# Output blocks of the third batch moved around the last attention, with another PE order

## The chip, the cores and the metric

The kernel runs on one core of one Trainium2 chip. The metric is the device time of one execution in microseconds. A core has TensorE (PE, with its weight loads as PEld), VectorE (DVE), ScalarE (ACT), GpSimd (POOL) and SyncE (SP), which issues the DMAs.

## What is computed

Inputs are q, k and v of 4 batches, 12 heads, 448 positions and 64 columns, in float32. Three stages follow one another in each batch:

```python
# 1: attention, causal, 12 heads -> x (448 x 768)
scores = q @ k.T / sqrt(64); scores[above the diagonal] = -1e9
x = softmax(scores) @ v
# 2: mixing of tokens and channels
theta = x @ w_theta
y = w_tok_r @ (x * cos(theta)) + w_tok_i @ (x * sin(theta))
u = x + y
x = u + relu(u @ w_ch)
# 3: four experts, each a causal attention; two per token count, by the gate
logits = x @ w_gate; w = softmax over the two largest of 4
out = sum over e of w[e] * (softmax(x wq[e] (x wk[e]).T / 8) @ (x wv[e])) @ wo[e]
```

## The kernel before, in words

Data lie transposed: 768 channels are six tiles of 128 partitions, 448 positions are the columns. Float32 products that have to be exact are made of a high and a low part in a rounded format, with three matmuls (high x high, high x low, low x high). Four kinds of work are recorded per batch b: `attn1` (a0 to a3: six pairs of heads, in three groups of two), `mixing` (m), `project` (p: the channel product, the queries and keys of the experts, the values and the gate) and `attn2` (c: two pairs of experts, then six output blocks).

Nothing is issued while it is recorded. `Plan` (line 187 on) keeps each operation as a step with what it reads and writes. PE's steps fall into 268 numbered places (`plan.next()`), and the list `RUNS` (line 568) says in which order PE takes them: (11,16) is the next 16 steps of place 11. `rank` derives a due time for every other step from PE's line, and `issue` runs a list schedule with these due times, in which it also chooses the engine of a step that has a choice (`copy` and `scale`, lines 302 to 316) and the buffer of each tile. The numbers in `K` (line 566) are margins of that schedule. Each engine then runs its instructions in the order so found.

Places that the text speaks of: 29 and 31 are mixing blocks of batch 0. 55 is the scores of the last 64 queries of the third group of `attn1(1)`, 57 the transposes of P of its last pair, 106 the first score place of `attn1(2)`. 171 is a mixing block of batch 2, 195 and 199 channel blocks behind it; 238 is the mixing block of batch 3's fifth tile and 241 a channel block. 214 and 215 are P times V of the third batch's `attn2`, 216 to 221 its output blocks. 251 to 254 are the values and the gate of batch 3, 255 to 257 the scores of the last `attn2`, 258 and 259 its transposes, 260 and 261 P times V, 262 to 267 its output blocks.

An output block (`attn2`, line 1064) is six matmuls with the attention output's high and low parts (`hl`), one eviction to SBUF (`ob`) by ScalarE or VectorE, and one store. Its weights are loaded into one of 4 buffers `c1` (for the last batch, of 6 buffers `unit`). In `two` (line 813) the gate enters through `norm` (line 762): the reciprocal of each row's sum is multiplied by the gate, and each tile of P is scaled by it before it is transposed by PE and copied from PSUM to SBUF. In `attn2` that scaling can run on GpSimd or ScalarE:

```python
    def scale(self, out, p, by, engines="gs"):
...
                plan.scale(p, p, rec[:, col:col + 1])
...
            hl = [sbt([S], F32R, "hc") for _ in range(2)] if x.dest is None else []
...
            ob = sbt([S], F32, "xt" if b == B - 1 else "cmb")
```

Pools have fixed numbers of buffers: hc 4, cmb 2, zt 10 (the pool of z), xt 12 (the pool of x). Two pairs of an `attn2` take all four of hc.

Of the kernel before, what the change touches and what calls it, by code (L numbers as in the profile page):

```python
# [12 lines left out]
F32 = mybir.dt.float32  # L13
F32R = mybir.dt.float32r
# [6 lines left out]
B, H, S, D = 4, 12, 448, 64  # L21
# [108 lines left out]
class Plan:  # L130
# [206 lines left out]
    def rank(self, last):  # L337
# [22 lines left out]
        for s in reversed(self.steps):  # L360
            if s.engine != "tensor":
# [3 lines left out]
                if s.engine == "sync":  # L365
                    s.after = max(0.0, s.due - K["ahold"])
        for group in groups.values():
# [187 lines left out]
class Engine:  # L555
# [7 lines left out]
BYDVE = {"a0": (), "a1": (), "a2": (0, 1, 2, 4, ), "a3": (0, 1, 2, 4, ), "c0": (0, 1, ), "c1": (0, 1), "c2": (0, 1, ), "c3": ()}  # L563
ZBYDVE = [(), (), (), ()]
ORDER = ["a0", "m0", "a1", "p0", "c0", "m1", "a2", "p1", "c1", "m2", "a3", "p2", "c2", "m3", "p3", "c3"]
K = {"path": 1.6514121, "hop": 476.4898, "slack": -38.9360047, "war": 176.7037, "ahold": 44547.6112,
    "free": -864.6802, "warm": 16}
RUNS = [(0,2), (1,2), (2,1), (8,2), (3,16), (7,2), (4,16), (9,1), (6,1), (5,1), (11,16), (14,2), (10,1), (22,1),
# [23 lines left out]

# [3 lines left out]
def dense_sparse_attention_kernel(ctx: ExitStack, tc: tile.TileContext, qk, v, w64, w32, wo, wvg, wtok, out):  # L596
# [6 lines left out]
    plan = Plan(nc, tc)  # L603
# [6 lines left out]
    def sbt(shape, dtype, tag):  # L610
        return plan.tile(sb, [P] + shape, dtype, tag, BUFS[tag])
# [98 lines left out]
    class Pair:  # L710


        def __init__(self, raw, vts, gate, dest, by_dve):
            self.fetch, self.vts, self.gate, self.dest, self.by_dve = raw, vts, gate, dest, by_dve

        def part(self, j, c):
            at = UNIT[c] + (c + 1) * j if c < 3 else UNIT[c]
# [44 lines left out]
        def norm(self, a, b_, items):  # L762
            rec, gate = self.rec, self.gate
            dve.tensor_scalar(rec[:, a:b_], self.sums[:, a:b_], 1e-9, None, op0=OP.add)
            dve.reciprocal(rec[:, a:b_], rec[:, a:b_])
            if gate is not None:
                dve.tensor_tensor(rec[:, a:b_], rec[:, a:b_], gate[:, a:b_], op=OP.mult)
            for p, col in items:
                plan.scale(p, p, rec[:, col:col + 1])

        def last(self, sc_):
            if self.by_dve:
# [40 lines left out]
    def two(pairs):  # L813


        for x in pairs:
            x.scores()
            x.soft(2)
            x.norm(0, 2, [(x.part(j, 2), j) for j in range(2)])
        plan.next()  # L820
        lasts = [pst("tp") for _ in range(2)]
        plan.group()
        for i in range(2):
            for j in range(2):
                pe.matmul(lasts[j][64 * i:64 * i + 64, :S], pairs[i].qs[j][:, 384:S], pairs[i].ks[j], start=True, stop=True)
        plan.end_group()
        for x, sc_ in zip(pairs, lasts):
            plan.completes(sc_[:, :S])
            plan.claim(x.p_)
        for x, sc_ in zip(pairs, lasts):  # L830
            x.last(sc_)
            x.soft(1)
            x.soft(0)
            x.norm(2, 7, [(x.part(0, 3), 6)] + [(x.part(j, c), 2 * (2 - c) + j) for c in (1, 0) for j in range(2)])
        for x in pairs:
            x.turn()
        got = []
        for i, x in enumerate(pairs):
            plan.next()
            o_ = pst("tp")  # L840
            hl = [sbt([S], F32R, "hc") for _ in range(2)] if x.dest is None else []
            plan.group()
            for kc in range(3):
                for j in range(2):
                    pe.matmul(o_[64 * j:64 * j + 64, kc * P:384], x.vts[j][:, kc], x.moving(kc, j, kc, 384 - kc * P), start=(kc == 0), stop=(kc == 2))
            for kc in range(4):
                for j in range(2):
                    pe.matmul(o_[64 * j:64 * j + 64, 384:S], x.vts[j][:, kc], pairs[j].moving(3, j, kc, 64, 64 * i), start=(kc == 0), stop=(kc == 3))
            plan.end_group()
            plan.completes(o_[:, :S])  # L850
            for tile_ in hl if x.dest is None else (x.dest,):
                plan.claim(tile_)
            if x.dest is not None:
                plan.copy(x.dest, o_[:, :S])
                continue
            h_, l_ = hl
            plan.copy(h_, o_[:, :S])
            dve.tensor_tensor(l_, o_[:, :S], h_.f32(), op=OP.subtract)
            got.append((h_, l_))
        return got  # L860
# [202 lines left out]

    def attn2(b):
        qps, v2, g7 = st2[b]
        hl = two([Pair(lambda r=r: qps[r], [v2[r][:, :, j] for j in range(2)], g7[:, r, :], None, r in BYDVE[f"c{b}"]) for r in range(2)])
        for m in range(NK):
            wu = unit(100 + m, 2 * P, 1, "unit" if b == B - 1 else "c1")[0].rearrange("p h (r j) -> p h r j", r=2)
            plan.next()
            ob = sbt([S], F32, "xt" if b == B - 1 else "cmb")  # L1070
            ends = [0, S // 2, S] if b == B - 1 and m == NK - 1 else [0, S]
            for lo, hi in zip(ends, ends[1:]):
                o = pst("tp")
                i = 0
                plan.group()
                for k in range(2):
                    for a, c in ((0, 0), (1, 0), (0, 1)):
                        pe.matmul(o[:, lo:hi], wu[:, a, k], hl[k][c][:, lo:hi], start=(i == 0), stop=(i == 5))
                        i += 1
                plan.end_group()  # L1080
                plan.claim(ob)
                plan.copy(ob[:, lo:hi], o[:, lo:hi])
                sp.dma_start(out[b, m * P:(m + 1) * P, lo:hi], ob[:, lo:hi])
# [7 lines left out]
    for what in ORDER:  # L1091
        kind, b = what[0], int(what[1])
# [43 lines left out]
```

## Time and profile before

| | |
|---|---|
| median of 3 runs | 605.19 us (605.19 to 605.22) |
| the profiled execution | 605.35 us, its span 603.6 us |
| granted TensorE clock | 1.000 of full speed |
| busy, share of the span | PE 98%, PEld 83%, DVE 69%, ACT 54%, POOL 18% |
| the chain that ended last | PE 82%, DVE 8%, ACT 7%, DMA 1%, issue 1% |
| HBM | 168 GB/s over the span |

The span runs from the first to the last instruction. Almost all operations are issued by one helper, so they have one line (L552) and are told apart by their tiles: `tp` and `mm` are PSUM tiles, `pa` is P, `ph` is P transposed, `st` small statistics, `hc` the attention output's parts, `zt` the tiles of z, `xt` those of x, `c` the pool c1, `unit` weights. A float32 matmul of two passes shows as two instructions.

### The profile page before, as it was taken

How to read it: one execution, taken by the hardware profiler on the slowest of the kernel's cores; microseconds unless marked ns; L12 is line 12 of the kernel's file. 1: busy time of each engine (PE TensorE's matmuls, PEld its weight loads, DVE VectorE, ACT ScalarE, POOL GpSimd, SP SyncE). 2: the span in 40 equal slices, each digit the busy share in tenths (PEclk: the TensorE clock that was granted, in tenths of full speed). 3: DMA queues.
4: the chain of work that ended last, by engine and by line, in shares of the span. 5: the costliest groups of instructions: out<-in, count | busy, mean ns of one | idle time of the engine just before them, and what ended most of it. 6: DMA issues, size and time to landing. Idle time of an engine off the chain costs nothing.

```text
span 603.6 us, 11721 instructions
## 1 busy us (share of the span) xinstructions
PE 590.8 (98%) x3950; PEld 499.1 (83%) x3950; DVE 414.0 (69%) x1268; ACT 323.0 (54%) x874; POOL 107.2 (18%) x201
## 2 busy tenths in 40 slices
PE   8999998999999999999999999999999999999987
PEld 6678786899898888987887888987878898899886
DVE  6899999999847889355638878537735866324261
ACT  5999899556435376055546545228535632100373
POOL 3542040010002131023300222012500203000020
PEclk9999999999999999999999999999999999999999
DMA  8357792079767566575667748385755846067442
GB/s 321 141 186 244 244 329 90 2 245 305 269 209 271 166 194 205 139 259 159 194 180 240 242 112 301 92 284 193 222 139 164 274 132 213 1 213 219 137 136 91
DMA packets 57851, 117.08 MB, mean 194 GB/s; under 512 B 8384, under 2 KB 21824, under 8 KB 57792
## 3 DMA queue, kind: packets, MB, share of 16 engines
q1 hardware_dynamic: 57792, 116.34, 60.3%
q8 instruction: 31, 0.51, 0.4%
q14 instruction: 28, 0.23, 0.1%
HBM read 80.37 MB, written 21.26 MB: 168 GB/s over the span
## 4 chain that ended last, share of the span: by engine, by line
PE 82%; DVE 8%; ACT 7%; DMA 1%; issue 1%; POOL 0%; SPq 0%; POOLq 0%; DVEq 0%; ACTq 0%
PE mm L552 56%; PE tp L552 26%; ACT pa L552 4%; DVE pa L552 2%; DVE zt L552 2%; ACT ph L552 1%; DMA unit<-scr 1%; ACT zt L552 1%; DVE cmb L552 1%; DVE st L552 1%; DVE tp L552 1%; ACT L552 0%; DVE ph L552 0%; DVE sm L552 0%; DMA ph<-pa 0%
## 5 line engine op out<-in xcount | busy, mean ns | idle before, releaser
L552 PE MATMUL mm<-zt,unit 128*128 128x448 f32 x1152 | 246.1, 369 | 2.6 <-DVE zt L552 1.4
L552 PEld LDWEIGHTS mm<-zt,unit 128*128 128x128 f32 x1152 | 213.7, 188 | 26.7 <-DVE zt L552 3.4
L552 ACT ACTIVATE pa<-pa,st 128x256 f32<-128x256 f32 (+4 forms) x238 | 115.2, 526 | 17.2 <-DVE st L552 16.1
L552 PE MATMUL mm<-wt,zh 128*128 128x448 f32 x336 | 98.8, 373 | 2.3 <-DVE wt L552 1.5
L552 POOL TENSOR_SCALAR pa<-pa,st 128x384 f32<-128x384 f32 (+4 forms) x112 | 60.4, 556 | 213.8 <-DVE st L552 147.6
L552 PEld LDWEIGHTS mm<-wt,zh 128*128 128x128 f32 x336 | 61.5, 188 | 11.4 <-DVE wt L552 3.2
L552 PE MATMUL tp<-raw 64*128 64x384 f32 (+3 forms) x512 | 67.6, 439 | 0.5 <-DVE st L552 0.5
L552 DVE CUSTOM_DVE_ANT_0 pa<-tp,mask 128x256 f32<-128x256 f32 (+3 forms) x126 | 50.2, 444 | 19.8 <-PE tp L552 19.7
L552 ACT ACTIVATE pa<-tp,st 128x256 f32<-128x256 f32 (+3 forms) x98 | 48.4, 506 | 28.0 <-DVE st L552 19.4
L552 PE MATMUL mm<-wt,zl 128*128 128x448 f32 x168 | 61.5, 366 | 0.1
L552 PEld LDWEIGHTS tp<-ph,vt 128*64 128x64 f32 x896 | 41.9, 137 | 23.4 <-issue 13.2
L552 PE MATMUL tp<-ph,vt 128*64 128x64 f32 (+3 forms) x896 | 60.7, 291 | 0.0
L552 PEld LDWEIGHTS tp<-raw 64*128 64x128 f32 (+1 forms) x512 | 38.9, 173 | 21.1 <-issue 5.4
L552 DVE CUSTOM_DVE_ANT_0 tp<-tp,mask 128x256 f32<-128x256 f32 (+3 forms) x98 | 42.2, 474 | 11.3 <-PE tp L552 7.4
L552 DVE SCALAR_TENSOR_TENSOR xt<-mm,xt 128x448 f32<-128x448 f32 x24 | 14.8, 618 | 41.5 <-PE mm L552 41.5
L552 DVE TENSOR_TENSOR zt<-xt,zt 128x448 fp32r<-128x448 f32 (+1 forms) x76 | 40.6, 570 | 0.4
L552 ACT ACTIVATE zh<-tp 128x384 fp32r<-128x384 f32 (+1 forms) x42 | 20.5, 537 | 35.6 <-PE tp L552 35.5
L552 ACT ACTIVATE cmb<-tp 128x448 f32<-128x448 f32 x15 | 8.1, 542 | 57.6 <-PE tp L552 57.6
L552 PE MATMUL tp<-ident,pa 128*128 128x128 f32 x288 | 36.0, 276 | 2.6 <-POOL pa L552 2.5
L552 PEld LDWEIGHTS tp<-ident,pa 128*128 128x128 f32 x288 | 31.7, 141 | 6.2 <-POOL pa L552 3.1
L552 DVE STREAM_TRANSPOSE pa<-pa 128x1024 f32<-128x1024 f32 x28 | 33.8, 1226 | 2.9 <-POOL pa L552 2.0
L552 DVE TENSOR_TENSOR xt<-xt,mm 128x448 f32<-128x448 f32 x24 | 14.8, 616 | 29.7 <-PE mm L552 29.7
(103 smaller groups left out, 723.0 us busy)
## 6 DMA issues: line engine op xcount, KB each, us to landing
unit<-scr SPq DMA_DIRECT2D x96, 384.0 KB, 4.2
ph<-pa SPq DMA_DIRECT2D x224, 64.0 KB, 2.0
scr<-unit SPq DMA_DIRECT2D x32, 384.0 KB, 3.6
raw<-qk SPq DMA_DIRECT2D x24, 448.0 KB, 5.0
c<-w SPq DMA_DIRECT2D x24, 384.0 KB, 3.8
vt<-v SPq DMA_DIRECT2D x24, 256.0 KB, 4.1
unit<-scr SPq DMA_DIRECT2D x18, 260.0 KB, 3.2
out<-cmb SPq DMA_DIRECT2D x18, 224.0 KB, 3.2
```

What stands on the lines that cost most here:

```text
L552: getattr(getattr(self.nc, engine), name)(*args, **kw)
```

## The change

The four edits of the code, and of the new list the parts that the text speaks of (the whole list is replaced):

```diff
-K = {"path": 1.6514121, "hop": 476.4898, "slack": -38.9360047, "war": 176.7037, "ahold": 44547.6112,
-    "free": -864.6802, "warm": 16}
+K = {"path": 1.2953704, "hop": 533.3355, "slack": -9.8564954, "war": 150.0, "ahold": 42013.9526, "free": -4199.9303,
+    "warm": 16}
...
-    (44,1), (24,14), (28,7), (27,7), (24,4), (26,18), (50,16), (49,16), (54,2), (31,3), (51,1), (106,1), (53,2),
-    (31,1), (29,10), (52,1), (31,17), (29,11), (32,7), (30,7), (35,21), (36,7), (55,1), (33,21), (34,7), (38,21),
-    (37,21), (63,18), (56,1), (61,18), (56,8), (62,18), (65,18), (57,16), (64,18), (56,7), (60,18), (58,1), (59,1),
+    (50,5), (28,6), (27,5), (25,1), (27,2), (26,18), (24,18), (49,9), (106,1), (49,7), (29,5), (53,1), (50,11),
+    (31,5), (51,1), (54,1), (53,1), (55,1), (29,10), (54,1), (52,1), (31,16), (29,6), (32,7), (30,7), (57,5),
+    (35,21), (34,4), (57,6), (33,21), (34,3), (36,7), (37,21), (38,21), (63,18), (62,18), (65,18), (57,5), (60,18),
...
-    (170,7), (147,1), (148,1), (166,6), (172,21), (169,21), (162,7), (154,1), (168,4), (165,21), (168,3), (171,21),
-    (199,18), (196,18), (152,1), (194,18), (181,2), (197,18), (180,2), (182,1), (179,1), (178,1), (188,2), (198,9),
+    (169,21), (162,1), (165,8), (195,2), (168,7), (165,13), (154,1), (171,21), (195,16), (197,18), (188,2), (180,2),
...
-    (236,21), (238,21), (220,1), (241,13), (240,18), (216,1), (244,18), (221,1), (243,18), (241,5), (242,18),
-    (245,18), (248,18), (249,18), (247,9), (246,18), (218,1), (247,9), (256,2), (255,2), (257,1), (253,18), (254,12),
-    (252,18), (251,18), (217,1), (219,1), (258,16), (259,16), (260,1), (261,1), (262,1), (265,1), (267,1), (264,1),
-    (263,1), (266,1), (267,1)]
+    (229,1), (238,1), (229,2), (232,21), (238,19), (241,18), (242,18), (240,18), (243,18), (245,18), (244,18),
+    (248,18), (249,18), (246,18), (247,18), (251,8), (256,1), (255,2), (256,1), (257,2), (253,18), (251,10),
+    (254,12), (252,18), (216,1), (221,1), (218,1), (258,16), (259,16), (217,1), (261,1), (260,1), (219,1), (220,1),
+    (265,1), (267,1), (264,1), (263,1), (266,1), (262,1)]
...
-        def __init__(self, raw, vts, gate, dest, by_dve):
-            self.fetch, self.vts, self.gate, self.dest, self.by_dve = raw, vts, gate, dest, by_dve
+        def __init__(self, raw, vts, gate, dest, by_dve, late=False):
+            self.fetch, self.vts, self.gate, self.dest, self.by_dve, self.late = raw, vts, gate, dest, by_dve, late
...
-                plan.scale(p, p, rec[:, col:col + 1])
+                plan.scale(p, p, rec[:, col:col + 1], "gsv" if self.late else "gs")
...
-            hl = [sbt([S], F32R, "hc") for _ in range(2)] if x.dest is None else []
+            hl = []
+            if x.dest is None and x.late:
+                both = sbt([960], F32R, "zt")
+                hl = [both[:, 0:S], both[:, 512:]]
+            elif x.dest is None:
+                hl = [sbt([S], F32R, "hc") for _ in range(2)]
...
-        hl = two([Pair(lambda r=r: qps[r], [v2[r][:, :, j] for j in range(2)], g7[:, r, :], None, r in BYDVE[f"c{b}"]) for r in range(2)])
+        hl = two([Pair(lambda r=r: qps[r], [v2[r][:, :, j] for j in range(2)], g7[:, r, :], None, r in BYDVE[f"c{b}"], b == B - 1) for r in range(2)])
...
-            ob = sbt([S], F32, "xt" if b == B - 1 else "cmb")
+            ob = sbt([S], F32, "xt" if b >= B - 2 else "cmb")
```

In the old order two output blocks of the third batch (217, 219) stand between the last values and the last transposes, and the other four stand earlier, between the channel blocks and the heads of batch 3. In the new order all six stand around the last attention: three ahead of its transposes, one between these and P times V, two behind that. For the last batch VectorE is a third choice for scaling P, the two parts of the attention output share one tile of the pool of z, and the third batch's output blocks are evicted to tiles of the pool of x.

## Rows read from the trace of the kernel before

**Rows 1.** The page, busy us (share of the span) xinstructions:
```profile
PE 590.8 (98%) x3950; PEld 499.1 (83%) x3950; DVE 414.0 (69%) x1268; ACT 323.0 (54%) x874; POOL 107.2 (18%) x201
```
**Rows 2.** Waits of PE: who <- for whom: us in total, times, longest:
```profile
PE tp L552 <- POOL pa L552: 2.5, 2, 1.7
PE mm L552 <- DVE wt L552: 1.5, 3, 0.6
PE mm L552 <- DVE zt L552: 1.4, 3, 0.7
```
**Rows 3.** Chain that ended last, tail: start us, us, what:
```profile
572.55 8.08 PE mm L552 x66
...
584.17 0.59 POOL pa L552
```
**Rows 4.** Timeline of PE, tail: start us, us, engine, line, op, out<-in, xcount:
```profile
526.47 1.39 PE L552 MATMUL tp<-hc,c 128*128 128x448 f32 x6
...
565.26 1.38 PE L552 MATMUL tp<-hc,c 128*128 128x448 f32 x6
...
580.46 2.63 PE L552 MATMUL tp<-hc,c 128*128 128x448 f32 x12
584.81 3.79 PE L552 MATMUL tp<-ident,pa 128*128 128x128 f32 x32 [1.73 <-POOL pa L552]
588.53 3.74 PE L552 MATMUL tp<-ph,vt 128*64 128x384 f32 x56
592.20 8.05 PE L552 MATMUL tp<-hc,unit 128*128 128x448 f32 x42
```
**Rows 5.** The same chain, earlier stretches of PE without a wait:
```profile
386.06 11.56 PE mm L552 x57
...
439.87 3.67 PE tp L552 x56
...
508.89 0.76 PE tp L552 x7
...
565.42 1.22 PE tp L552 x6
```
**Rows 6.** Instructions on P's tile, 583 to 604 us: duration ns min/median/max:
```profile
L552 ACT ACTIVATE pa<-pa,st x7: 387/493/663, 584.1 to 586.8; 128x384 f32<-128x384 f32 x2, 128x256 f32<-128x256 f32 x2, 128x128 f32<-128x128 f32 x2, 128x448 f32<-128x448 f32 x1
L552 POOL TENSOR_SCALAR pa<-pa,st x7: 371/480/641, 584.2 to 587.2; 128x384 f32<-128x384 f32 x2, 128x256 f32<-128x256 f32 x2, 128x128 f32<-128x128 f32 x2, 128x448 f32<-128x448 f32 x1
```
**Rows 7.** Groups of VectorE by shape, whole span: busy us, mean ns | idle before:
```profile
L552 DVE COPY ph<-tp 128x512 f32<-128x512 f32 x19 | 12.3, 680 | 1.3 <-PE tp L552 1.3
...
L552 DVE CUSTOM_DVE_ANT_0 pa<-tp,mask 128x448 f32<-128x448 f32 x18 | 10.7, 616 | 0.6 <-PE tp L552 0.6
...
L552 DVE TENSOR_SCALAR unit<-cmb 128x384 fp32r<-128x384 f32 x5 | 1.7, 346 | 0.0
```
**Rows 8.** Timeline of the weight loads, behind the last transposes and P times V:
```profile
588.53 0.20 PEld L552 LDWEIGHTS tp<-ph,vt 128*64 128x64 f32 x4 [0.17 <-ACT ph L552]
...
592.92 0.30 PEld L552 LDWEIGHTS tp<-hc,unit 128*128 128x128 f32 x2 [0.21 <-ACT hc L552]
593.58 6.49 PEld L552 LDWEIGHTS tp<-hc,unit 128*128 128x128 f32 x37 [0.36 <-DVE hc L552]
```
**Rows 9.** Timeline of ScalarE and VectorE, tail: an eviction and a subtraction:
```profile
583.12 0.54 ACT L552 ACTIVATE cmb<-tp 128x448 f32<-128x448 f32 x1 [0.37 <-PE tp L552]
...
592.90 0.62 DVE L552 TENSOR_TENSOR hc<-tp,hc 128x448 fp32r<-128x448 f32 x1 [1.14 <-ACT hc L552]
```
**Rows 10.** Timeline of PE, behind the last P times V of batch 3's attention:
```profile
471.42 5.95 PE L552 MATMUL mm<-zt,unit 128*128 128x448 f32 x28 [0.67 <-DVE zt L552]
```
**Rows 11.** The output blocks' weight tile, 500 to 604 us: its loads:
```profile
DMA to landing us min/median/max: 2.8/5.4/7.5
```
**Rows 12.** Busy us of each engine in stretches of 50 us (xinstructions), clock, DMA:
```profile
50.00:100.00 50.00, 48.90 (x352) 39.52 (x353) 49.90 (x154) 47.28 (x124) 10.12 (x21) 1.00 0.71 243
100.00:150.00 50.00, 48.77 (x279) 42.75 (x276) 49.19 (x125) 33.20 (x75) 4.51 (x8) 1.00 0.47 162
```

More of the change, by code (lines that the diff above doesn't have):

```diff
@@ L565 @@
 ORDER = ["a0", "m0", "a1", "p0", "c0", "m1", "a2", "p1", "c1", "m2", "a3", "p2", "c2", "m3", "p3", "c3"]
-K = {"path": 1.6514121, "hop": 476.4898, "slack": -38.9360047, "war": 176.7037, "ahold": 44547.6112,
-    "free": -864.6802, "warm": 16}
-RUNS = [(0,2), (1,2), (2,1), (8,2), (3,16), (7,2), (4,16), (9,1), (6,1), (5,1), (11,16), (14,2), (10,1), (22,1),
[23 rows of a table removed]
+K = {"path": 1.2953704, "hop": 533.3355, "slack": -9.8564954, "war": 150.0, "ahold": 42013.9526, "free": -4199.9303,
+    "warm": 16}
+RUNS = [(0,2), (1,2), (2,1), (8,2), (3,16), (7,2), (4,16), (9,1), (6,1), (5,1), (11,16), (14,1), (22,3), (14,1),
[24 rows of a table added]
 @with_exitstack
```

30 rows, old and new, of the table RUNS are left out of this document.

## The prediction

> **What bounds the kernel now.** I read the views in this order: the engine shares, the waits of PE, the chain that ended last, and then the timeline of the last 25 us. PE is the busiest engine by far: it stands still for 603.6 - 590.8 = 12.8 us [rows 1], of which 3.35 lie behind its last matmul at 600.25 [rows 4], so 9.4 are left. The reader should see in [rows 2] that the longest single wait of PE is 1.7 us, that it is for GpSimd's scaling of P, and that the next two are for VectorE. In the chain of waits [rows 3] PE's own work stands end to end almost everywhere. So a time can only fall where PE stands still, and the change moves PE's work without adding or taking any: the same 3950 matmuls run. The tail shows where it stands still. The value blocks end at 572.55 + 8.08 = 580.63; two output blocks of the third batch follow; the first transpose of P starts at 584.81 [rows 3, 4]. Between lies the gate: copy of the logits, rank, exponential, normalisation on VectorE and ScalarE, and the first scaling of P on POOL (584.17, 0.59 us). That chain is 584.81 - 580.63 = 4.18 us long and does not depend on PE. PE has two blocks in it and idles 1.73 us.
>
> **The rates used.** One output block (six matmuls) takes 1.22 us of the chain; seven transposes 0.76, so 0.109 each; 56 matmuls of P times V 3.67; 57 matmuls of 448 columns 11.56, so 0.203 each [rows 5].
>
> **The change part by part.**
>
> *(a) A third block before the transposes.* The new order runs places 216, 221 and 218 between the values and the transposes where the old one ran 217 and 219. The gate chain stays as long as it is, so 1.22 us of the 1.73 are filled and 0.5 us stay: -1.22. The idle was cover that nobody used, so nothing is lost by it; next in line stays the gate chain. Bounds: -1.73 (the chain also gets shorter, see b) and -0.2 (two evictions, 0.54 us each on ScalarE [rows 9], come ahead of the scales). I take -1.22, since the row of the block is exact and the old evictions already ran beside this chain.
>
> *(b) VectorE may scale P of the last pairs.* In the tail 14 tiles are scaled, 7 on POOL at 0.37 to 0.64 us [rows 6] and 7 on ScalarE. VectorE is not shown scaling P; the nearest row is its scaling from SBUF to SBUF of the same 384 columns, 0.35 us [rows 7], against POOL's 0.59 for the first. So the first transpose could come up to 0.24 us earlier, or, if a scale on VectorE stands ahead of one of its copies of transposed P, 0.35 us later. I take 0: the transposes use up a scaled tile about as fast as two engines make them, and VectorE is the engine that copies.
> What two engines do to each other here has no row: VectorE does no SBUF work in place while POOL scales in the tail. The Trainium skill (SBUF — State Buffer, section "SBUF: two separate sides") says that VectorE and GpSimd share one pair of ports as an exclusive lock, taken for a whole instruction by a VectorE operation in a two-port mode. By that rule a VectorE scale would wait for POOL's, at most one of 0.64 us, and the sum below would be smaller by that at worst; no run so far shows it.
>
> *(c) A block between the transposes and P times V (217), two behind P times V (219, 220).* PE takes 588.53 - 584.81 = 3.72 us for 32 transposes [rows 4], worth 32 x 0.109 = 3.49; at the seam the weight load waits 0.17 us for the last copy of transposed P [rows 8]. Block 217 covers that: -0.15 (bounds -0.25 and 0). Behind P times V, the first final block waits for the high part and then the low part of the attention output, 0.21 + 0.36 us on the weight loads [rows 8]. With 219 and 220 there (2.44 us) the copy of 0.54 and the subtraction of 0.62 [rows 9], 593.58 - 592.27 = 1.3 us in all, fit in: -0.5 (bounds -0.6 and -0.3; the last is if an eviction of 219 goes ahead of the copy).
>
> *(d) What the four blocks leave behind.* Before, 220, 216, 221 and 218 stood between 526 and 566 us; the first and the last of the four are shown [rows 4]. 220 stood between the last mixing block and the first channel block of batch 3. Now channel block 241 follows directly on mixing block 238, whose tile it reads as its fifth of six: at its 13th matmul, 12 x 0.203 = 2.44 us later. In batch 2 the old order already had that distance (mixing 171, then channel 199), and the 57 matmuls there ran in one piece [rows 5]: cost 0. The other bound is the wait at 471.42 us, 0.67 us for VectorE at that same distance behind an attention block, where VectorE was full [rows 10]. In batch 2 the new order runs two matmuls of 195 early, so only 10 x 0.203 = 2.03 us lie behind 171: 0.2 taken, bounds 0 and 1.1. Together +0.2.
>
> *(e) The blocks' other instructions.* Each moved block brings one eviction (0.54 us) and one store of 224 KB, and a load of its weights into one of four buffers. Loads 5 and 6 can start only when 216 and 221 are done, near 583 us; they land within 7.5 us [rows 11], near 590.5, and their readers come 8.4 us of PE work after the first transpose, near 592.5. Cover 2 us, cost 0; if it went, the wait would be for one load, up to the 2 us by which it could be late. On SP's queue they stand behind the six loads of the last batch's weights, which wait for the same value blocks. The tiles from the pools of x and z only remove waits: the third batch's high and low parts hold all four old buffers until its last block, and without another pool the last attention would wait for them.
>
> *(f) The order planned anew elsewhere.* The PE order differs from the first microseconds on. PE's sum of work is the same, so only waits change, and I found none that is removed on purpose. The sensitive stretch is 50 to 150 us, where VectorE is busy 49.9 and 49.2 of 50 us [rows 12] and PE waits for the mixing weights (DVE wt, 1.5 us) [rows 2]. The new order asks for the last score block of batch 1's third group (place 55) before mixing instead of in the middle of it, and for transposes of that group (57) between mixing blocks; in return half of batch 2's first scores (106) leaves the stretch. I take 0; the bounds are -1.5 (those waits go) and +3.3 (worked out below).
>
> **The sum.** -1.22 + 0 - 0.15 - 0.5 + 0.2 + 0 + 0 = -1.67 us. The profiled execution took 605.35 us, its span 603.6 and 1.75 around it; the end behind the last matmul (eviction, store, close) is the same work. That gives a span of 601.9 and 603.7 in all for a run like the profiled one, which is 0.16 us above the median shown; against the median, 605.19 - 1.67 = 603.5 us.
>
> **The rivals.**
> 1. *The tail gains and the early stretch gains too.* PE's waits for the mixing weights shrink because more PE work stands ahead of the last of them. For it: the new order splits mixing blocks 29 and 31 into pieces of 5, 10, 6 and 5, 16 with other work between. Against: VectorE makes these weights and is full. 603.5 - 1.5 = 602.0 us or a little less.
> 2. *The idle is filled, but the gate chain moves out by as much.* In the same 4 us ScalarE and VectorE now also evict three blocks (3 x 0.54), and the scales and the copies of transposed P follow. If two evictions stand ahead of the scales, 1.1 us of (a) are gone: 605.19 - 0.57 = 604.6 us, no change that counts.
> 3. *Slower.* Place 55 is brought ahead of the mixing, and VectorE does its two last score rows (0.61 us each) and the three copies of transposed P that place 57 needs (0.68 each) [rows 7] before the mixing weights: 1.2 + 2.0 = 3.3 us, all on PE's path as VectorE has no free time there: 603.5 + 3.3 = 606.8 us. From 2.9 us on it makes the kernel slower by more than 0.2%. For it: VectorE's share. Against: ScalarE can take the copies, and half a score block leaves.
> 4. *The change does less than it says:* the plan never lets VectorE scale, and only the order counts. That costs nothing here, as (b) stands at 0.
>
> **How the numbers follow.** A measurement of this kernel tells about 0.2%, 1.2 us, from no change: faster is under 603.98, slower over 606.40. My forecast (602.6 to 604.4) has 0.48, of which 0.41 is below 603.98; rival 1 has 0.13, rival 2 0.21, rival 3 0.18. So faster 0.41 + 0.13 = 0.54, same 0.07 + 0.21 = 0.28, slower 0.18. The range runs from rival 1 with (a) at its better bound, 601.2, to just short of rival 3, 606.6.
>
> **What would show it.** (a) holds if PE's wait for the scales of the last P is 0.3 to 0.7 us; it fails if the first transpose comes more than 4.5 us behind the last value matmul. (c) holds if the weight loads behind P times V show no wait. (d) fails if PE waits more than 0.3 us for VectorE's halves right behind mixing block 171 or 238. (f) shows in PE's busy time by stretches of 50 us: over 1.5 us less than before in 50 to 150 us is rival 3, as much more is rival 1. The prediction is wrong if PE's idle time ahead of 560 us changes by more than the tail's does.

## The result and the profile after

The changed kernel takes 598.65 us (median of 3 runs, 598.33 to 599.14) against 605.19 us before: ratio 0.9893, 95% interval 0.987 to 0.9915. That is 6.5 us less where 1.7 were forecast, and below the range of 601.2 to 606.6. The profiled execution took 598.33 us with a span of 596.3.

The page after, busy times (answers [rows 1]), and PE's waits (answer [rows 2]; us in total, times, longest):

```profile
PE 587.7 (99%) x3950; PEld 499.1 (84%) x3950; DVE 419.2 (70%) x1288; ACT 325.4 (55%) x876; POOL 93.6 (16%) x179
```
```profile
PE mm L552 <- POOL ident masks.py:199: 1.4, 1, 1.4
PE tp L552 <- POOL pa L552: 0.7, 1, 0.7
PE tp L552 <- DVE zl L552: 0.7, 1, 0.7
PE tp L552 <- DVE st L552: 0.7, 2, 0.5
PE mm L552 <- DVE zt L552: 0.5, 2, 0.3
...
PE mm L552 <- DVE wt L552: 0.2, 1, 0.2
```

The 1.7 us wait for GpSimd's scaling is gone, and so are most of the waits for the mixing weights (`wt`). The timeline of PE in the tail after (answers [rows 4]):

```profile
570.25 3.83 PE L552 MATMUL tp<-hc,c 128*128 128x448 f32 x18
574.32 3.73 PE L552 MATMUL tp<-ident,pa 128*128 128x128 f32 x32 [0.24 <-DVE pa L552]
577.80 1.47 PE L552 MATMUL tp<-hc,c 128*128 128x448 f32 x6
579.21 3.74 PE L552 MATMUL tp<-ph,vt 128*64 128x384 f32 x56
582.88 2.71 PE L552 MATMUL tp<-hc,c 128*128 128x448 f32 x12
585.43 7.57 PE L552 MATMUL tp<-zt,unit 128*128 128x448 f32 x42
```

And the busy times by stretch, from 50 to 150 us (answer [rows 12]): PE is the first engine, VectorE the third. PE is busy 98.87 us here where it was 97.67.

```profile
50.00:100.00 50.00, 49.06 (x351) 39.38 (x349) 49.55 (x146) 49.34 (x120) 10.02 (x21) 1.00 0.76 248
100.00:150.00 50.00, 49.81 (x286) 45.49 (x287) 48.20 (x123) 32.49 (x79) 5.44 (x10) 1.00 0.58 192
```

**Where the time went.** Busy times hide much of it: a matmul of 448 columns is shown busy for 0.37 us, while the next one can start 0.206 us behind it, so gaps between starts need not show as idle time. So I use PE's *lag*: the moment at which PE starts an instruction, less 1.36 us (its first start) and less what all instructions before it in its own order take back to back, each with the median start-to-start interval of its form in the trace before (0.206 us for 448 columns, 0.119 for 260, 0.109 for a transpose, 1.861 for P times V of a pair). The total is 575.8 us in both orders. Growth of the lag in us, by stretch of that back-to-back time (counted from the span's start, the 1.36 us included):

| kernel | 5 to 116 | of that 80 to 105 | 116 to 320 | 320 to 506 | 506 to 576 (tail) |
|---|---|---|---|---|---|
| before | 11.58 | 5.13 | 4.17 | 2.30 | 2.69 |
| after | 8.76 | 1.29 | 2.19 | 2.15 | 0.55 |
| old head, new tail | 11.51 | 5.16 | 4.22 | 2.30 | 1.12 |
| new head, old tail | 8.53 | 1.08 | 2.19 | 2.18 | 1.82 |
| the same, old code | 8.99 | 1.54 | 2.35 | 2.13 | 2.15 |
| old order, new code | 11.56 | 5.16 | 4.37 | 2.30 | 2.28 |
| old order, new margins | 18.69 | 10.24 | 3.31 | 2.84 | 2.49 |
| new order, old margins | 28.94 | 19.14 | 11.04 | 2.89 | 0.65 |

After against before: -2.82, -1.98, -0.15 and -2.14, together -7.1 of the 7.3 us between the spans. The tail gave 2.1 us; 5 us came from the head. The stretch from 80 to 105 us of PE's work, which is batch 0's mixing at 89 to 119 us of the trace before, gave 3.8 us by itself; the rest of 5 to 116 us lost 1.0.

### The profile page after: what moved, and what is told of

Read it like the earlier page. It is cut to its first block, busy times and chain, and to the rows that moved or that the text cites. A ratio compares the mean times of both kernels' runs of the same rounds, so it can differ in the third digit from the quotient of the medians.

```text
span 596.3 us, 11696 instructions
## 1 busy us (share of the span) xinstructions
PE 587.7 (99%) x3950; PEld 499.1 (84%) x3950; DVE 419.2 (70%) x1288; ACT 325.4 (55%) x876; POOL 93.6 (16%) x179
## 4 chain that ended last, share of the span: by engine, by line
PE 79%; DVE 9%; ACT 8%; DMA 2%; issue 1%; POOL 0%; POOLq 0%; DVEq 0%; ACTq 0%
PE mm L552 56%; PE tp L552 24%; ACT pa L552 4%; DVE pa L552 3%; DVE zt L552 2%; ACT zt L552 1%; DMA zt<-wtok 1%; ACT L552 1%; DVE cmb L552 1%; DVE ph L552 1%; ACT ph L552 1%; DMA unit<-scr 1%; DVE st L552 1%; ACT c L552 0%; DVE sm L552 0%
## 5 line engine op out<-in xcount | busy, mean ns | idle before, releaser
L552 ACT ACTIVATE pa<-pa,st 128x384 f32<-128x384 f32 (+3 forms) x230 | 111.7, 526 | 49.0 <-DVE st L552 26.4
L552 POOL TENSOR_SCALAR pa<-pa,st 128x384 f32<-128x384 f32 (+4 forms) x108 | 57.3, 547 | 194.4 <-DVE st L552 100.7
L552 PE MATMUL tp<-raw 64*64 64x448 f32 (+3 forms) x512 | 68.0, 438 | 0.5 <-DVE st L552 0.5
L552 PEld LDWEIGHTS tp<-ph,vt 128*64 128x64 f32 x896 | 42.0, 137 | 23.3 <-issue 13.5
L552 ACT ACTIVATE zh<-tp 128x512 fp32r<-128x512 f32 (+1 forms) x43 | 22.2, 548 | 41.5 <-PE tp L552 36.6
L552 DVE SCALAR_TENSOR_TENSOR xt<-mm,xt 128x448 f32<-128x448 f32 x24 | 14.9, 621 | 37.1 <-PE mm L552 37.1
L552 DVE TENSOR_TENSOR zt<-xt,zt 128x448 fp32r<-128x448 f32 (+1 forms) x81 | 39.2, 528 | 0.4
L552 PEld LDWEIGHTS mm<-wt,zl 128*128 128x128 f32 x168 | 31.6, 188 | 4.4 <-DVE zl L552 1.2
L552 PE MATMUL mm<-unit,zt 128*128 128x260 f32 (+1 forms) x264 | 34.2, 285 | 0.0
```

The costliest lines, as they stand in the source:

```text
L552: getattr(getattr(self.nc, engine), name)(*args, **kw)
```

## The experiments

All were timed beside the kernel before on the same chip (605.0 to 605.7 us there); ratios come with 95% intervals. "Head" is all up to the last mixing block of batch 3 (place 238), where both orders have issued the same steps; "tail" is the rest.

**Old head, new tail** (code edits in, old margins):

```diff
     ... old list up to (238,21),
-    (220,1), (241,13), (240,18), (216,1), (244,18), (221,1), ...
+    (241,18), (242,18), (240,18), (243,18), (245,18), (244,18), ...
```


> PE's old order up to the last mixing block of batch 3, then the new order from the channel blocks of batch 3 on; code edits in, old margins. Theory (two separate gains: the tail's by the moved blocks, about 2.4 us by PE's lag behind its own work from 560 us on, and the head's by the new order): 605.2 - 2.4 = 602.8 us. Rival 1 (the gain is the head's alone, the tail's stall only moves): 605 us. Rival 2 (the tail's blocks bring it all, the head follows from them): 599 us.

Measured: 604.49 us, ratio 0.9988 (0.9978 to 0.9998). Its lag is the kernel's before up to 506 us, then 1.12 instead of 2.69: the new tail takes 1.6 us from the trace. The timed gain is 0.8 us (0.1 to 1.3 by the interval), about half of that. The start scatters by as much (last section), but the medians of 10 and 19 executions stand against each other here, and why they show less than the trace is not known. Expected were 2.4.

**New head, old tail** (code edits in, new margins): the new list up to (238,19), then (220,1), (241,13) and so on as before.

> The new order up to the last mixing block of batch 3, then the old order of the tail; code edits in, new margins. Theory: only the head's gain, 605.2 - 4.5 = 600.7 us, and PE waits 1.4 to 1.7 us again before the last transposes. Rival 1: 598.7 us. Rival 2: 605 us.

Measured: 599.50 us, ratio 0.9915 (0.9883 to 0.9947). So the head brings most of it. PE's wait before the transposes is back; the first row is this kernel's timeline, the second that of old head and new tail:

```profile
578.44 3.73 PE L552 MATMUL tp<-ident,pa 128*128 128x128 f32 x32 [1.44 <-DVE pa L552]
```
```profile
580.05 4.00 PE L552 MATMUL tp<-ident,pa 128*128 128x128 f32 x32 [0.20 <-DVE pa L552]
```

**The code edits alone** (old order, old margins; the diff of the document ahead without K and RUNS).

> The old order of PE and the old margins, with the code edits (VectorE as a third choice for the last scales, the parts of the last attention output in the pool of z, the third batch's output tiles in the pool of x). Theory: only the first scale is faster, by 0.2 to 0.3 us: 604.9 to 605.2 us. Rival (the pools free the plan everywhere): 603 us or less.

Measured: 605.34 us, ratio 1.0003 (0.9991 to 1.0016): no change that can be timed. In the trace the tail's lag is 2.28 instead of 2.69.

**The new head without the code edits** (new margins, old tail):

> PE's new order up to the last mixing block of batch 3, the old one for the tail, the new margins, and none of the code edits. Theory (the head's gain is the order and margins found together; the code edits only matter in the tail): 599.5 us, as with the code edits. Rival (the third batch's output tiles and the freed pool let the head's plan be what it is): 602 us or more.

Measured: 600.86 us, ratio 0.9934 (0.9911 to 0.9957); the lag over 5 to 506 us is 13.5 us, against 12.9 with the code edits and 18.1 before. All but 0.6 us of the head's gain is there without the code edits: it comes from the order and the margins.

**VectorE not allowed to scale:**

```diff
-                plan.scale(p, p, rec[:, col:col + 1], "gsv" if self.late else "gs")
+                plan.scale(p, p, rec[:, col:col + 1], "gs")
```


> The changed kernel with the last scales left to GpSimd and ScalarE. Theory: the first scale takes 0.59 us instead of 0.34, so PE waits 0.2 to 0.4 us more before the last transposes: 598.9 to 599.1 us. Rival (VectorE's scaling, 12 of 14 tiles, carries the transposes): 599.7 us or more, with PE waiting inside the transposes too.

Measured: 598.26 us, ratio 0.9884 (0.9868 to 0.9901): no loss that can be timed. In the trace the wait before the transposes is 0.47 us instead of 0.24, as the first theory has it, and nothing else waits:

```profile
574.08 3.73 PE L552 MATMUL tp<-ident,pa 128*128 128x128 f32 x32 [0.47 <-ACT pa L552]
```

**A fourth block ahead of the transposes:**

```diff
-    (258,16), (259,16), (217,1), (261,1), ...
+    (217,1), (258,16), (259,16), (261,1), ...
```


> The changed kernel with place 217 ahead of the last transposes too, so four output blocks stand there and none between the transposes and P times V. Theory: PE's last wait for the gate chain (0.24 us) goes, and a wait for the last copy of transposed P of 0.2 to 0.3 us comes back at the seam: 598.4 to 598.8 us, no change that counts. Rival (the seam is the dearer place, since ScalarE makes 7 of the 8 copies there): 599.5 us or more.

Measured: 599.08 us, ratio 0.9901 (0.9884 to 0.9917). The wait for the gate chain went, and one of 0.88 us at the seam came: dearer than I thought, cheaper than the rival. The time can't be told from the changed kernel's.

```profile
579.73 3.74 PE L552 MATMUL tp<-ph,vt 128*64 128x384 f32 x56 [0.88 <-DVE ph L552]
```

**Order or margins?** Four kernels exchange one of the two. First, only K in the kernel before; second, only K in the changed kernel:

```diff
-K = {"path": 1.6514121, "hop": 476.4898, "slack": -38.9360047, "war": 176.7037, ...
+K = {"path": 1.2953704, "hop": 533.3355, "slack": -9.8564954, "war": 150.0, ...
```


> The kernel before with nothing changed but the schedule's margins K. Theory (PE's new order makes the head's gain of about 5 us of PE's lag): 605 us, within 0.5 either way. Rival (the margins set the order on VectorE and ScalarE, and that makes the gain, PE's order only follows): 601 to 602.5 us, with the lag over 80 to 105 us of PE's work falling from 5.1 us to under 2.

> The changed kernel with the old margins K. Theory (PE's order): 598.7 to 599.5 us. Rival (margins): most of the head's gain goes, 602 us or more; and if the order found with other margins does not fit these, slower still.

Third, the new order up to batch 0's last mixing block in the kernel before; fourth, the old order up to there in the changed kernel:

> The kernel before, with PE's new order up to the last mixing block of batch 0 and the old one for what is left; old margins, none of the code edits. Theory (half of batch 2's first scores out of the stretch, other work between the two first mixing blocks): PE's lag over 5 to 116 us of its work falls from 11.6 us to about 8.8, time 602.4 us. Rival (margins): lag 11 us or more, 605 us.

> The changed kernel with PE's old order up to the last mixing block of batch 0; new margins and code edits. Theory: lag over 5 to 116 us is back at about 11.6 us, time 598.65 + 2.8 = 601.5 us. Rival (margins): it stays under 9.5 us, 599 us.

Measured: 613.75 us (ratio 1.0133, 1.0103 to 1.0163), 627.23 (1.0359, 1.0319 to 1.04), 616.85 (1.0191, 1.0161 to 1.0221) and 612.62 (1.0121, 1.0098 to 1.0143). Theory and rival both fell: neither the order nor the margins carry the gain. Each is worth something only with the other, and without it the lag grows by 10 to 19 us over 80 to 105 us of PE's work alone. Part of that is the clock: in all four the granted clock fell to half in this stretch, in or right behind PE's long waits (mean over the profiled executions 0.978 to 0.994; last section). PE's waits in the third kernel (60 to 140 us), then in the fourth:

```profile
PE mm L552 <- ACT wt L552: 9.9, 2, 9.1
PE tp L552 <- DVE zl L552: 1.4, 1, 1.4
PE mm L552 <- DVE wt L552: 1.0, 2, 0.8
```
```profile
PE tp L552 <- ACT pa L552: 7.3, 1, 7.3
PE mm L552 <- ACT wt L552: 1.3, 1, 1.3
```

PE takes its list strictly in order. With the new order it asks for mixing weights early; with the old margins ScalarE and VectorE make them late, and PE stands for 9.1 us. The high half of the third weight is the one it stands for: ScalarE makes it at 107.4 us in the third kernel and at 92.4 in the changed one (timelines of ScalarE, in this order):

```profile
107.41 0.56 ACT L552 ACTIVATE wt<-cmb 128x448 fp32r<-128x448 f32 x1
```
```profile
92.40 0.60 ACT L552 ACTIVATE wt<-cmb 128x448 fp32r<-128x448 f32 x1
```

With the old order and the new margins it is a transpose that waits 7.3 us for ScalarE's P.

**Single edits in batch 0's mixing.** Half of place 106 moved out of it in the kernel before; the high halves of the mixing weights kept off VectorE there; both:

```diff
-    ... (51,1), (106,1), (53,2),
+    ... (51,1), (53,2),
...
-    ... (58,1), (59,1),
+    ... (58,1), (59,1), (106,1),
```
```diff
-            plan.copy(hi, p_, "sgv")
+            plan.copy(hi, p_, "sg" if hi.root.tag == "wt" else "sgv")
```


> The kernel before with one entry of PE's order moved: the second half of place 106 (batch 2's first scores) goes behind P times V of batch 1's last group, out of batch 0's mixing; margins and code as before. Theory (VectorE is full in the stretch, and the four masks of these scores, 0.36 us each, stand ahead of the mixing weights): PE's lag over 80 to 105 us of its work falls from 5.1 to about 3.7 us, time 603.8 us. Rival (only an order and margins found together fit; any single edit lets another engine come late): 607 us or more.

> The kernel before with the high halves of the mixing weights kept off VectorE (before: 3 of 7 there, 0.38 us each); order and margins as before. Theory (VectorE full): 1.1 us less lag over 80 to 105 us, time 604.1 us. Rival (ScalarE is as full and each copy there is 0.58 us and comes later): 605.2 to 606.5 us.

> The kernel before with both edits, the half score place moved out of batch 0's mixing and the high halves of the mixing weights off VectorE. Theory: the two add up, 2.5 us less lag, time 602.7 us. Rival (fit): 607 us or more.

Measured: 609.60 us (ratio 1.0068, 1.0051 to 1.0086), 607.71 (1.004, 1.0027 to 1.0053) and 608.06 (1.0048, 1.0029 to 1.0066), with 8.4, 8.1 and 9.0 us of lag over 80 to 105. Taking work off the full engine made the stretch worse each time, as the rival has it. But the clock has a share in it. In every execution of these three the mean granted clock was 0.991 to 0.997; in the traces it fell to half for 3.4, 3.4 and 6.8 us at some 105 to 113 us, where the kernel before kept 1.00. Over those us the lag grew by some 1.5, 1.7 and 3.2 us more than PE's recorded waits. So of the second kernel's 2.3 us the larger part may be the clock's, and what the edits cost by the plan alone is not separated. The stretch from 105 to 108 us before, then with both edits (the clock is the number behind POOL's):

```profile
105.00:108.00 3.00, 3.00 (x14) 2.42 (x14) 2.38 (x8) 2.16 (x5) 0.00 (x0) 1.00 0.00 0
```
```profile
105.00:108.00 3.00, 2.09 (x4) 1.02 (x5) 3.00 (x7) 2.98 (x13) 0.00 (x0) 0.50 0.00 0
```

The reverse in the changed kernel, with "gv" for the mixing weights:

> The changed kernel with the high halves of the mixing weights kept off ScalarE (6 of 7 there); order and margins as in the changed kernel. Theory: VectorE or GpSimd takes them, up to 6 x 0.38 = 2.3 us more on VectorE: 600 to 601 us. Rival (fit): 605 us or more with one wait of PE of 5 us or longer.

Measured: 601.93 us, ratio 0.9942 (0.9922 to 0.9962); the lag over 80 to 105 is 3.95 us instead of 1.29, and PE waits 1.6 us for VectorE's halves. This one went the way that the theory of a full VectorE has it, by 0.9 us more than its upper end.

**Another staging tile.** A mixing weight is put together in a tile of cmb (2 buffers), which it shares with the channel weights:

```diff
-        p_ = sbt([S], F32, "cmb")[:, :n]
+        p_ = (sbt([S], F32R, "hc").f32() if hi.root.tag == "wt" else sbt([S], F32, "cmb"))[:, :n]
```


> The kernel with the new early order and the old margins (616.9 us), where the mixing weights' staging tile comes from the pool hc (4 buffers, not used until batch 0's last stage) instead of the two buffers of cmb that they share with the channel weights. Theory (two channel weights hold both cmb buffers while the last mixing weights wait): the 9.1 us wait of PE goes to under 2 us, 608 us or less. Rival (the weights come late by the order of VectorE's and ScalarE's due times, whatever the buffers): the wait stays over 6 us, 614 us or more.

> The kernel before with the mixing weights' staging tile from the pool hc; order and margins as before. Theory (in the kernel before the shared cmb buffers delay the mixing weights too): lag over 80 to 105 us of PE's work falls from 5.1 us to 3 or less, 603 us. Rival (VectorE is the limit there and the plan fits the old staging): 605 us or more.

> The changed kernel with the mixing weights' staging tile from the pool hc. Theory: the first two weights come early already, little is left: 598 to 599 us. Rival (fit): 601 us or more.

Measured: 609.57 us (ratio 1.0069, 1.005 to 1.0087) where 616.85 stood; 604.15 (0.9982, 0.997 to 0.9994); 599.42 (0.9911, 0.9887 to 0.9935). In the first the 9.1 us wait fell to 4.5:

```profile
PE mm L552 <- ACT wt L552: 4.5, 1, 4.5
```

So up to half of that wait was for staging buffers, as far as one kernel with a new plan can tell; both answers are half right. In the other two kernels the stretch of 80 to 105 us got no better: 5.36 us of lag instead of 5.13, and 3.27 instead of 1.29. The second is a little faster by 116 to 320 us, where its lag is 2.86 instead of 4.17 us, though the edit touches nothing there but what the plan makes of it.

No version tried is measurably faster than the changed kernel.

## Why the prediction was wrong

The tail, by the prediction's steps:

- *(a) Third block before the transposes:* right. The wait fell from 1.73 to 0.24 us, 1.49 less; forecast were 1.22 and, with (b) at its better bound, 1.46. (It lies just below the 0.3 to 0.7 us that the prediction names as its sign, by what (b) gave.) The chain after, from the last value matmul (563.33 + 7.09 = 570.42) to the first transpose (574.32), is 3.90 us, against 4.18 by [rows 3, 4]:

```profile
563.33 7.09 PE mm L552 x58
...
573.93 0.34 DVE pa L552
```

- *(b) VectorE scales:* taken at 0, worth 0.23 us (0.47 against 0.24 above). In the tail it scales 12 of 14 tiles and GpSimd none, so they do not meet there. The rule on their ports that the prediction takes from the Trainium skill (SBUF — State Buffer, section "SBUF: two separate sides") is shown by no run here. Instructions on P's tile after (answers [rows 6]; ns min/median/max):

```profile
L552 DVE TENSOR_SCALAR pa<-pa,st x12: 277/346/448, 573.9 to 577.2; 128x256 f32<-128x256 f32 x4, 128x384 f32<-128x384 f32 x3, 128x128 f32<-128x128 f32 x3, 128x448 f32<-128x448 f32 x2
L552 ACT ACTIVATE pa<-pa,st x2: 388/502/615, 573.9 to 574.4; 128x384 f32<-128x384 f32 x1, 128x128 f32<-128x128 f32 x1
```

- *(c) Blocks behind the transposes:* the final blocks take 7.57 instead of 8.05 us and no weight load waits behind P times V, -0.48 for -0.5. At the seam only 0.05 came of 0.15: from the first transpose to P times V are 579.21 - 574.32 = 4.89 us, less 1.22 for the block 3.67, against 3.72.
- *(d) What the blocks leave behind:* PE has no recorded wait from 380 to 392 us or from 517 to 560; 0 instead of +0.2.
- *(e) Their loads and stores:* no wait; right.

So the sum for the tail, -1.67, stands against -1.57 with the old head (1.12 - 2.69), -1.27 between new head with old tail and the changed kernel (0.55 - 1.82), and -2.14 in all. By the trace the mechanism and the size were right; that the timed gain of the tail by itself was only 0.8 us stays open.

**The step that failed is (f):** "I take 0; the bounds are -1.5 (those waits go) and +3.3". The head gave -4.95 us (11.58 + 4.17 + 2.30 against 8.76 + 2.19 + 2.15). Of the signs that the prediction set for it, PE's busy time in 50 to 150 us rose by 1.2 us only and pointed to no rival; PE's idle time ahead of 560 us fell from 7.7 to 5.1 us, more than behind it (5.1 to 3.5), and did say that it is wrong. That the time fell, as forecast, is for 5 of the 7 us the work of a term put at nothing: so far the direction is luck. (The range's lower end is 601.5 by its own terms, not 601.2.) Two things were wrong in (f).

First, the better bound was read from PE's wait rows: 1.5 us for the mixing weights. Over 80 to 105 us of PE's work the lag grew by 5.1 us. Much of the rest lay in starts that were spread while PE is shown busy, 48.8 of 50 us from 100 to 150 us by [rows 12], and in waits that the profile puts on the weight loads. Those could be read ahead of time: from 60 to 112 us PE's weight loads waited 3.2 us for VectorE's mixing weights before (first row) and 1.0 after.

```profile
PEld mm L552 <- DVE wt L552: 3.2, 5, 0.9
```
```profile
PEld mm L552 <- DVE wt L552: 1.0, 2, 0.6
```

Rows of VectorE in the timeline, the mixing weights' low halves, first before, then after, show why the first matmuls waited: the second weight came at 94.5 us before, at 87.5 after.

```profile
88.93 0.61 DVE L552 TENSOR_TENSOR wt<-cmb,wt 128x448 fp32r<-128x448 f32 x1
94.50 0.62 DVE L552 TENSOR_TENSOR wt<-cmb,wt 128x448 fp32r<-128x448 f32 x1
...
104.97 0.61 DVE L552 TENSOR_TENSOR wt<-cmb,wt 128x448 fp32r<-128x448 f32 x1
```
```profile
86.41 0.62 DVE L552 TENSOR_TENSOR wt<-cmb,wt 128x448 fp32r<-128x448 f32 x1
87.47 0.62 DVE L552 TENSOR_TENSOR wt<-cmb,wt 128x448 fp32r<-128x448 f32 x1
...
103.82 1.15 DVE L552 TENSOR_TENSOR wt<-cmb,wt 128x448 fp32r<-128x448 f32 x2
```

The last weight comes at nearly the same time in both. After, PE has ten matmuls of two mixing blocks done on the first weights, with scores and transposes between them, and only 0.2 us left to wait for a weight. That fits rival 1's mechanism, at -3.8 us where it was priced at -1.5; no run separates the split mixing blocks from the weights that come earlier. ScalarE makes six of the seven high halves there, three before; in the run that kept them off ScalarE 2.7 us of the lag came back.

Second, I priced the order by PE's line alone. The exchanges show that it has no price by itself: the same order with the other margins costs 28.6 us more than with its own. Rival 3 took one consequence of the new order, more work on VectorE ahead of the weights, as if the plan around it stayed.

**What stays open.** The 1.98 us of 116 to 320 us lie in many small steps: PE's recorded waits from 125 to 335 us are 1.1 us before and 0.2 after, none over 0.5. No run names a cause for them. A changed staging tile alone moved that stretch by 1.3 us, so such sums may follow from any replanning. Nor do the runs separate PE's order from the order on the other engines within a plan: that would need the order of every engine carried over from one plan to the other with its buffers, and was not tried.

## What to carry to other kernels

When a change replaces a planned order, price the whole order: its parts have no value alone, and an exchange of the margins alone cost the two kernels 9 and 29 us here. Read what a bound engine can still gain from its start-to-start intervals against a steady stretch, not from its recorded waits; the waits of PE for the weights named 1.5 us where the lag grew by 5. Look at the granted clock of a stretch before its lost time is put down to an edit. And split a mixed change at a place where both orders have issued the same work: two runs told the head from the tail.

## What was not expected of the hardware

A long wait can cost twice. In the kernel with the new early order and old margins PE stood still from 98.9 to 108 us, and the granted clock fell from 1.00 (2.4 GHz) to 0.50 (1.2 GHz); it stayed there to 116 us while PE worked on with short waits. Busy times by stretch, the clock is the first number behind POOL's:

```profile
98.00:101.00 3.00, 0.95 (x9) 0.19 (x1) 3.00 (x15) 2.98 (x6) 0.00 (x0) 1.00 0.71 259
101.00:104.00 3.00, 0.00 (x0) 0.00 (x0) 3.00 (x8) 2.99 (x7) 0.00 (x0) 0.73 0.00 0
104.00:107.00 3.00, 0.00 (x0) 0.00 (x0) 3.00 (x9) 3.00 (x10) 0.00 (x0) 0.50 0.45 117
...
113.00:116.00 3.00, 3.00 (x13) 1.98 (x14) 2.96 (x7) 1.94 (x6) 0.00 (x0) 0.50 0.01 3
```

A matmul of 448 columns then took 0.57 us or more instead of 0.37, and the lag grew by 14.9 us over 80 to 105 us of work, where PE's waits for the weights name 10.9. In the three kernels with single edits the clock fell with no wait of PE over 1.8 us ahead of it: several shorter ones stood close together there.

The start scatters. PE's lag after its first 5 us of work was between 1.41 and 2.92 us in the profiled executions, with the same first instructions on PE; from there to 506 us the kernel before, old head with new tail and old order with new code run alike within 0.2 us (18.05, 18.03 and 18.23 by the table), and so do the changed kernel and new head with old tail (13.10 and 12.90). That is why differences under 1 us are read here from the lag behind the start and not from the total; but each such figure is from one trace.
